# PSUM as eight banks with a fixed plan, and a fixed order of issue, in a sliding-window attention with a gated feed-forward layer

## The chip, the cores and the metric

The kernel runs on one core of a Trainium2 chip. The core has five engines that work side by side, each through its own instructions in order: TensorE (PE in the profile, with its weight loads as PEld), VectorE (DVE), ScalarE (ACT), GpSimd (POOL) and SyncE (SP). POOL and SP also issue the DMA transfers between the memory of the chip (DRAM) and the on-chip buffer (SBUF). Matmuls write to PSUM, a second on-chip buffer of 128 partitions and eight banks; a bank holds 512 fp32 values of each partition. The metric is the device time of one execution in microseconds (us).

## The reference

```python
batch, n_heads, seq, head_dim = (8, 8, 576, 64)          # q, k, v

scores = scale * np.matmul(q, k.transpose(0, 1, 3, 2))    # scale = 1 / sqrt(64)
rel = pos[:, None] - pos[None, :]
slopes = 2.0 ** (-8.0 * (np.arange(H) + 1) / H)
mask = (rel >= 0) & (rel < 128)
scores = np.where(mask, scores - slopes * np.abs(rel), -1e9)
attn = softmax(scores) @ v

x = attn_out.transpose(0, 2, 1, 3).reshape(B * S, H * D)  # 4608 x 512
H = np.maximum(x @ w_h, 0.0)
T = sigmoid(x @ w_t + b_t)
out = T * H + (1.0 - T) * x
```

The inputs and the output are fp32. A query sees itself and the 127 keys before it, with a penalty that grows with the distance.

## The kernel before

**Tiles.** Two batch elements are worked on together (`m` = 0 to 3). The 576 positions of each are four blocks of 128 and a tail of 64. Attention of a pair comes in stages. For m = 1 to 3 they are A (key blocks 0 and 1) and B (2, 3 and the tail); for m = 0 they are the four quarters a, b, c and d. Each stage has eight heads, taken as four pairs `g`. Rows of 128 tokens of a finished stage then go through the feed-forward part, one group at a time: 36 groups in all.

**Pieces.** The work is cut into 763 pieces, called nodes in the code, each of which belongs to one engine:
- On POOL: the loads `qk` (q or k, cast to bf16 while they are moved), `tl` (their tails), `v` (one chunk of 128 keys for both batch elements and all heads, to the tile `VA[m % 2]`), `w` (weights and bias); later `t` (the gate's scaling) and `o` (the output sum).
- On SP: `wf`, the load of w_h in fp32 into a staging area that is the q buffer of m = 1 (`QL[1]`, L215), and the stores `st`.
- On PE: `tr` transposes q (w = 0) or k (w = 1) through PSUM; `s` computes scores of a head (of two heads for m = 0); `pv` multiplies the softmax numerators with V for two heads; `xp` transposes a group of x, `h` and `z` are its two matmuls of 512 columns.
- On ACT: `wc` casts w_h from the staging area to bf16, `te` moves transposes of k from PSUM to SBUF, `exp` is the softmax numerator, `x` moves the transposed x, `th` is the tanh that stands for the sigmoid.
- On DVE: `te` moves transposes of q (and some of k), `msk` multiplies the numerators with the mask, `nrm` divides by the softmax sum, `u` and `g` are parts of the gate, and several memsets and tables of constants run at the start. Among these `ones` (L180) sets the last of the 65 columns that each head has in `VA`, in all five chunks by one memset: the extra column makes `pv` produce the softmax sum. `v` loads fill the other 64 columns of one chunk each.

**Order.** `plan` (L698) is a list scheduler: it holds a cost and a priority for every piece, models buffers, engines and loads, and hands back an order. `SHIFT` and `LOOKS` tune it. The pieces are then issued in that order under `manual_schedule`, so that every engine runs its own pieces in it. A layer below adds the semaphore waits by itself: a piece waits for the earlier pieces that touched the same part of a tile, as far as that layer can tell the parts apart.

**PSUM.** One pool `ps` of four buffers, each of two banks (L78). Every use takes a whole buffer through `ps_tile`: scores of one head, the two transposes of a q and k part (q in the first half, k in the second), and also a group's `xp`, `h` and `z`, which fill one bank of it. A buffer is taken in turn, when the piece that held it four uses earlier is done with it.

**Loads.** The order on POOL's queue before is: q, k, q, k quarters of m = 0; the other halves of q and k of m = 0; q and k of m = 1 whole; w_t, bias; tails of m = 0; V chunks 0 and 1; tails of m = 1; V chunks 2, 3, 4; V of m = 1; q, k and tails of m = 2; V of m = 2; and so on. Eight semaphores serve these transfers in turn, so that a load is issued when the load eight places before it has landed. A load to a buffer that is in use also waits for the last reader.

Of the kernel before, what the change touches and what calls it, by code (L numbers as in the profile page):

```python
# [14 lines left out]
def kernel(  # L15
# [50 lines left out]
        "ps": 4, "pA": 5, "pB": 4, "x": 3, "xt": 5, "uu": 3, "tt": 3, "ot": 3,  # L66
# [11 lines left out]
    psp = ctx.enter_context(tc.tile_pool(name="ps", bufs=BUFS["ps"], space=PSUM))  # L78

    def ps_tile(dt=F32):  # L80
        return psp.tile([P, 2, 512 if dt == F32 else 1024], dt, name="ps")
# [51 lines left out]
    MKA = cp.tile([P, H, 2 * P], BF16, name="mka")  # L133
# [114 lines left out]
    def transposes(m, w, part):  # L248
        i = m % 2
        if w == 0:  # L250
            TR[m, part] = ps_tile(BF16)
        pt = TR[m, part][:, w, :]
# [23 lines left out]
    def evac(m, w, part):  # L276
        i = m % 2
        pt = TR[m, part][:, w, :]
# [24 lines left out]
    def scores(m, kind, h):  # L303
        i, W = m % 2, width(kind)
        if W == 512 or h % 2 == 0:
            SC[m, kind, h] = ps_tile()
        else:
            SC[m, kind, h] = SC[m, kind, h - 1]
# [62 lines left out]

    def pv(m, kind, g):
        va = VA[m % 2]
        av = ps_tile()
# [45 lines left out]
    def f_x(m, kind, gi):  # L420
        bs, n, x = grp(m, kind, gi)
        pt = ps_tile(BF16)
        TR[m, kind, gi] = pt
        for i in range(n):
            for c in range(NCK):
                nc.tensor.transpose(  # L426
                    out=pt[:, i, c * P : (c + 1) * P], in_=x[:, i, c * P : (c + 1) * P],
                    identity=ident[:],
                )

    def f_xe(m, kind, gi):
        n = grp(m, kind, gi)[1]
        xt = fx.tile([P, 2, NCK, P], BF16, name="xt")
        XT[m, kind, gi] = xt
        nc.scalar.copy(  # L435
            out=xt[:, 0:n].rearrange("p i c n -> p i (c n)"), in_=TR[m, kind, gi][:, 0:n, 0:512]
        )

    def f_h(m, kind, gi, i):
        if i == 0:  # L440
            AH[m, kind, gi] = ps_tile()
        for c in range(NCK):
            nc.tensor.matmul(out=AH[m, kind, gi][:, i, :], lhsT=XT[m, kind, gi][:, i, c, :],  # L443
                             rhs=wH[:, c, :], start=c == 0, stop=c == NCK - 1)

    def f_u(m, kind, gi):
# [4 lines left out]
            out=uu[:, 0:n, :], in0=AH[m, kind, gi][:, 0:n, :], scalar=0.0, in1=x,  # L451
# [3 lines left out]
    def f_z(m, kind, gi, i):  # L455
        if i == 0:
            AZ[m, kind, gi] = ps_tile()
        az = AZ[m, kind, gi][:, i, :]
# [5 lines left out]
    def f_th(m, kind, gi):  # L464
# [3 lines left out]
        nc.scalar.activation(out=tt[:, 0:n, :], in_=AZ[m, kind, gi][:, 0:n, :], func=ACTF.Tanh,  # L468
# [34 lines left out]
    nodes = {}  # L503

    def node(key, eng, cost, prio, emit, deps=(), take=None, uses=(), land=0, n=1):


        nodes[key] = (eng, cost, prio, emit, [d for d in deps if d in nodes],
                      take, tuple(uses), land, n)
# [6 lines left out]
    node("ident", "POOL", 500, -120, c_ident)  # L516
    node("trim", "DVE", 300, -110, c_trim)
    node("tri", "POOL", 600, -96.5, lambda: c_tri(0), ["trim"])
    node("tri2", "POOL", 500, -80, lambda: c_tri(1), ["trim"])
    node("cbias", "ACT", 1500, -88, c_bias, ["ident"])  # L520
    node("mka", "DVE", 1300, -95, c_mka, ["tri"])
    node("cvec", "DVE", 1300, -90, c_vec)
    node(("ones", 0), "DVE", 300, -85, lambda: c_ones(0))
    node("mask0", "DVE", 1900, -50, lambda: c_mask(0), ["tri", "cvec"])
    node("mask1", "DVE", 1500, 5 * T, lambda: c_mask(1), ["tri", "tri2", "cvec"])
# [6 lines left out]
    def EV(m, w, part):  # L532
# [4 lines left out]
    HALF = {"A": (330, 1118, 1340, 470, 950), "B": (340, 1118, 1340, 900, 1080),  # L537
            "a": (210, 690, 790, 150, 640), "b": (210, 690, 790, 280, 640),
            "c": (210, 690, 790, 280, 640), "d": (250, 690, 790, 600, 800)}
# [7 lines left out]
    for m in range(ND):  # L547
        p0 = starts[m]
# [11 lines left out]
        def vv(*cs):  # L560
            for c in cs:
                seq.append((("v", m, c), 1150, 2000 if c < 4 else 1000, 1,
# [24 lines left out]
        for n, part in enumerate(parts):  # L587
            for w in (0, 1):
                if part == "tail":
                    src, cost, pr = ("tl", m, w), 450, p0 + (5 if m == 0 else 0 if len(parts) > 5 else -6) * T  # L590
                elif part[0] is None:
                    src, cost, pr = ("qk", m, w, None, None), 580, p0 + (2.4 * n - 12) * T
                else:
                    src, cost = ("qk", m, w, part[0], None if part[0] else part[1]), 1150
# [5 lines left out]
                     [src, "ident"] + [("tr", m, 0, part)] * w, take="ps" if w == 0 else None)  # L600
                node(("te", m, w, part), e, EVC[e][w] if part != "tail" else (420, 590)[e == "ACT"], pr + 1,
                     lambda m=m, w=w, part=part: evac(m, w, part),
                     [("tr", m, w, part)] + last_pv.get(m - 2, []), uses=[("tr", m, 0, part)])
        for kind in ORDER[m]:
            W, U, C = width(kind), UNIT[kind], HALF[kind]
            js = sorted({j for j, _, _ in STAGES[kind]})
            qs = sorted({qb for _, qb, _ in STAGES[kind]})
            for g in range(H // 2):
# [15 lines left out]
                for hl in range(2):  # L624
                    h = 2 * g + hl
                    tk = ("s", m, kind, h if W == 512 else 2 * g)
                    if tk[3] == h:
# [3 lines left out]
                             need + ["mka", "ident"] * add, take="ps")  # L631
                    node(("exp", m, kind, h), "ACT", C[1], tg + (hl - 1.2) * U,
                         lambda m=m, kind=kind, h=h: soft(m, kind, h), [tk, "cbias"] + [("exp", m, kind, 2 * g)] * hl + [owner] * (c0 > 0),
# [3 lines left out]
                if not add:  # L637
                    done = [("msk", key)]
                    node(("msk", key), "DVE", C[2], tg + U, lambda key=key: mask(*key),
                         exps + ["mask0"] + ["mask1"] * (kind in "Bd"), uses=[owner])  # L640
# [5 lines left out]
                     + [("vpad", m % 2)] * (4 in js) + [("v", m, c) for c in vs_], take="ps",  # L646
# [9 lines left out]
            for gi, bs in enumerate(GROUPS[kind]):  # L656
# [4 lines left out]
                if stage_no in DMA_X:  # L661
                    node(("x", kb), "SP", 450 * n, t - 1.3 * dt, lambda kb=kb: f_xd(*kb), alln,
                         take="xt", uses=[xo], land=1000 * n)
                else:
                    node(("xp", kb), "PE", 350 * n, t - 1.0 * dt, lambda kb=kb: f_x(*kb), alln,
                         take="ps", uses=[xo])
                    node(("x", kb), "ACT", (590, 1020)[two], t - 0.9 * dt, lambda kb=kb: f_xe(*kb),
                         [("xp", kb)], take="xt", uses=[("xp", kb)])
                for i in range(n):
                    node(("h", kb, i), "PE", 820, t + 0.4 * i * dt, lambda kb=kb, i=i: f_h(*kb, i),  # L670
                         [("x", kb), ("wc",), ("h", kb, 0)][: 2 + i], take=None if i else "ps",
                         uses=[("x", kb)])
                node(("u", kb), "DVE", (690, 1220)[two], t + 0.2 * dt, lambda kb=kb: f_u(*kb),
                     [("h", kb, n - 1)], take="uu", uses=[("h", kb, 0), xo])
                for i in range(n):
                    node(("z", kb, i), "PE", 1090, t + (0.5 + 0.4 * i) * dt,
                         lambda kb=kb, i=i: f_z(*kb, i),
                         [("x", kb), ("w", 1), ("w", 2)] + [("z", kb, 0)] * i,
                         take=None if i else "ps", uses=[("x", kb)])
# [15 lines left out]
                     lambda kb=kb: f_st(*kb), [("o", kb)], uses=[("o", kb)], land=650 * n)  # L695
            stage_no += 1

    def plan(shift, look):  # L698
        sync, land_ns = 90, 2000
        prio = {key: nd[2] + T * shift.get(key[0] if type(key) is tuple else key, 0.0)  # L700
                for key, nd in nodes.items()}
        when, order = {}, []
        clock = {e: 0.0 for e in ("PE", "ACT", "DVE", "POOL", "SP")}
        held, rings = {}, {r: [] for r in BUFS}
        users, waiting = {}, {}
        for key, nd in nodes.items():
            waiting[key] = len(nd[4])
            for d in nd[4]:
                users.setdefault(d, []).append(key)
            for o in nd[6]:  # L710
                held.setdefault(o, [0, 0.0])[0] += 1

        data = {key: 0.0 for key in nodes}
        ready = {e: [key for key, nd in nodes.items() if nd[0] == e and not nd[4]] for e in clock}
        queue, lanes = 0.0, [0.0] * 8
        while len(order) < len(nodes):
            best = None
            slot = {None: 0.0}
            for r, taken in rings.items():
                slot[r] = 0.0  # L720
                if len(taken) >= BUFS[r]:
                    left, at = held[taken[-BUFS[r]]]
                    slot[r] = None if left else at + sync
            for e in clock:
                cands = []
                for key in ready[e]:
                    nd = nodes[key]
                    s_ = slot[nd[5]]
                    if s_ is None:
                        continue  # L730
                    t = max(clock[e], data[key], s_)
                    if nd[7] and e == "POOL":
                        t = max(t, lanes[nd[8] - 1] + sync)
                    cands.append((t, prio[key], key))
                if cands:
                    t0 = min(c[0] for c in cands) + look[e]
                    c = min((c for c in cands if c[0] <= t0), key=lambda c: c[1])
                    if best is None or c[0] < best[0]:
                        best = c
            assert best, "no piece can start"  # L740
            t, _, key = best
            e, cost, _, _, _, take, uses, land, _ = nodes[key]
            if take:
                rings[take].append(key)
            clock[e] = when[key] = t + cost
            if land:

                shared = 3 * land if queue > t + cost + land else land
                queue = max(queue, t + cost) + land
                when[key] = (queue if e == "POOL" else t + cost + shared) + land_ns  # L750
                if e == "POOL":
# [53 lines left out]
```

The softmax here doesn't subtract the row's maximum and nothing guards it: scores larger than these inputs give would overflow.

## Time and profile before

| | us |
|---|---|
| median of three runs | 185.97 |
| lowest, highest | 184.8, 186.7 |
| the profiled execution | 185.63 |
| its span, first to last instruction | 183.9 |
| ACT exp, 80 instructions (L344) | 73.4 busy |
| PE `h` and `z`, 144 + 144 + 36 matmuls (L443, L460, L462) | 37.2 + 38.0 + 13.9 busy |
| DVE mask, 40 instructions (L363) | 47.8 busy |
| POOL output sum, 35 instructions (L484) | 49.7 busy |

The profile is of one execution; its span is 1.7 us shorter than the time of the same run. A page gives the busy time of each engine, a picture of the span in 40 slices (each digit is a busy share in tenths), the waits by the instruction that waited and the one that released it, the costliest groups of instructions, and the DMA issues with their time to landing. A time line lists instructions with start and duration. Matmul ends are modelled, so the distance of starts in the time line says more of PE's speed than the durations do.

### The profile page before, as it was taken

The page shows a single profiled execution, that of the slowest core. Times are in us where ns is not written, and L with a number is a line of the kernel's source. Part 1 is how long each engine was busy: PE and PEld are TensorE (multiplying, and loading weights), DVE is VectorE, ACT ScalarE, POOL GpSimd, SP SyncE. Part 2 cuts the span into 40 slices and gives each one's busy share as a digit, 9 for nine tenths or more (in the row PEclk, how much of TensorE's full clock was granted, in tenths as well). Part 3 has the DMA queues.
Part 4 walks back from the last instruction along what each step waited for, and adds up shares of the span by engine and source line. Part 5 has one row for each costly group of instructions (what it writes and reads, how often), then busy time and mean ns, then how long its engine had stood idle before and what let it go on. Part 6 is the DMA issues. An engine that isn't in the chain of part 4 may idle for free.

```text
span 183.9 us, 5244 instructions
## 1 busy us (share of the span) xinstructions
PE 155.0 (84%) x2132; PEld 93.9 (51%) x2132; DVE 141.6 (77%) x253; ACT 127.8 (69%) x178; POOL 121.5 (66%) x132
## 2 busy tenths in 40 slices
PE   0286886779999957997999999999998999999950
PEld 0264655655564524675554565665444666555510
DVE  5339885699999893697688999799899788866770
ACT  2558595753889953879779889786998888445510
POOL 7994123979999945984269953544487787667540
PEclk9999999999999996999999999999999999999995
DMA  4999999999999999999997994142212322243543
GB/s 157 225 187 198 200 199 176 138 132 92 127 207 228 210 200 205 135 187 225 208 135 96 178 159 90 45 103 61 57 45 74 93 66 74 74 103 99 137 128 94
DMA packets 70167, 25.50 MB, mean 139 GB/s; under 512 B 48128, under 2 KB 65024, under 8 KB 70144
## 3 DMA queue, kind: packets, MB, share of 16 engines
q0 software_dynamic: 62832, 14.68, 113.6%
q1 hardware_dynamic: 7312, 10.49, 21.3%
q8 instruction: 16, 0.26, 0.6%
q14 instruction: 7, 0.06, 0.1%
HBM read 30.41 MB, written 9.44 MB: 217 GB/s over the span
## 4 chain that ended last, share of the span: by engine, by line
PE 38%; DMA 26%; DVE 16%; POOL 7%; ACT 5%; issue 3%; SPq 1%; POOLq 0%; DVEq 0%; ACTq 0%
DMA kl<-in_k_dram 24%; PE ps L460 10%; PE ps L443 9%; DVE pt L363 6%; PE ps L386 6%; PE ps L270 5%; PE ps L328 5%; DVE x L403 4%; POOL ot L484 3%; DMA out_dram<-ot 3%; ACT pt L344 2%; PE ps L462 2%; DVE uu L450 2%; POOL ql L110 2%; PE ps L426 2%
## 5 line engine op out<-in xcount | busy, mean ns | idle before, releaser
L344 ACT ACTIVATE pt<-ps,bias 128x1024 bf16<-128x1024 f32 (+1 forms) x80 | 73.4, 951 | 9.1 <-PE ps L328 8.4
L484 POOL TENSOR_TENSOR ot<-uu,x 128x512 f32<-128x512 bf16 x35 | 49.7, 1421 | 30.4 <-DVE uu L478 28.9
L363 DVE TENSOR_TENSOR pt<-pt,mk 128x2048 bf16<-128x2048 bf16 (+1 forms) x40 | 47.8, 1210 | 0.7 <-ACT pt L344 0.5
L460 PE MATMUL ps<-wT,xt 128*128 128x512 bf16 x144 | 38.0, 387 | 1.2 <-DVE uu L450 0.7
L443 PE MATMUL ps<-wH,xt 128*128 128x512 bf16 x144 | 37.2, 380 | 0.6 <-DVE uu L450 0.3
L122 POOL DMA_DIRECT2D va<-in_v_dram x20 | 22.2, 1117 | 14.3 <-DMA kl<-in_k_dram 8.2
L450 DVE SCALAR_TENSOR_TENSOR uu<-ps,x 128x512 bf16<-128x512 f32 x36 | 24.8, 688 | 7.7 <-PE ps L443 7.3
L468 ACT ACTIVATE tt<-ps 128x512 f16<-128x512 f32 x36 | 21.5, 598 | 11.6 <-PE ps L462 11.1
L328 PE MATMUL ps<-qt,kt 64*128 64x256 bf16 (+2 forms) x384 | 27.2, 254 | 1.8 <-DVE kt L295 1.4
L473 POOL TENSOR_SCALAR tt<-tt 128x512 f16<-128x512 f16 x32 | 23.1, 722 | 5.6 <-ACT tt L468 5.5
L435 ACT COPY xt<-ps 128x512 bf16<-128x512 bf16 x36 | 21.0, 586 | 8.1 <-PE ps L426 7.2
L403 DVE TENSOR_TENSOR x<-ps,rd 128x256 bf16<-128x256 f32 (+3 forms) x40 | 25.5, 637 | 1.4
L386 PEld LDWEIGHTS <-pt 128*128 128x128 bf16 (+1 forms) x576 | 21.2, 101 | 8.0 <-issue 1.8
L386 PE MATMUL ps<-va,pt 128*128 128x65 bf16 (+1 forms) x576 | 24.1, 196 | 1.3 <-ACT kt L295 0.4
L295 ACT COPY kt<-ps 128x1024 bf16<-128x1024 bf16 x13 | 13.1, 1012 | 14.4 <-PE ps L270 8.4
L289 DVE COPY qt<-ps 128x1024 bf16<-128x1024 bf16 x16 | 10.9, 687 | 14.2 <-PE ps L270 10.9
L478 DVE TENSOR_TENSOR uu<-uu,tt 128x512 bf16<-128x512 bf16 x36 | 16.6, 462 | 4.9 <-POOL tt L473 2.9
L270 PE MATMUL ps<-ident,ql 128*64 128x128 bf16 (+1 forms) x320 | 13.3, 242 | 8.3 <-DMA ql<-in_q_dram 7.5
L443 PEld LDWEIGHTS <-xt 128*128 128x128 bf16 x144 | 12.1, 97 | 14.4 <-issue 2.8
L460 PEld LDWEIGHTS <-xt 128*128 128x128 bf16 x144 | 12.4, 99 | 13.7 <-issue 3.9
L328 PEld LDWEIGHTS <-kt 64*128 64x128 bf16 x384 | 12.8, 97 | 12.6 <-issue 7.0
L270 PE MATMUL ps<-ident,kl 128*64 128x128 bf16 (+1 forms) x320 | 12.8, 242 | 6.6 <-DMA kl<-in_k_dram 5.6
(46 smaller groups left out, 127.9 us busy)
## 6 DMA issues: line engine op xcount, KB each, us to landing
out_dram<-ot SPq DMA_DIRECT2D x128, 64.0 KB, 1.8
va<-in_v_dram POOLq DMA_DIRECT2D x16, 256.0 KB, 10.8
ql<-in_q_dram POOLq DMA_DIRECT2D x3, 1024.0 KB, 14.6
kl<-in_k_dram POOLq DMA_DIRECT2D x3, 1024.0 KB, 18.8
ql<-in_moe_w_h_dram SPq DMA_DIRECT2D x1, 1024.0 KB, 5.8
out_dram<-ot SPq DMA_DIRECT2D x8, 128.0 KB, 2.4
ql<-in_q_dram POOLq DMA_DIRECT2D x4, 128.0 KB, 5.8
kl<-in_k_dram POOLq DMA_DIRECT2D x4, 128.0 KB, 5.9
```

The costliest lines, as they stand in the source:

```text
L122: nc.gpsimd.dma_start(out=VA[m % 2][0:n, c, :, :, 0:D].rearrange("s r h d -> s (r h) d"), in_=v[2 * m : 2 * m + 2, :, c * P : c * P + n, : ...
L270: nc.tensor.transpose(out=pt[r * D : (r + 1) * D, c : c + n], in_=L[ps, r, nh * hs + hl, t * D : (t + 1) * D], identity=ident[ps, ps],)
L328: nc.tensor.matmul(out=sc[:, r, o + off : o + off + w_], lhsT=KT[i][rows, h, j * P : (j + 1) * P], rhs=rhs, start=not add, stop=not add or ...
L344: nc.scalar.activation(out=PT[m, home, h // 2][:, h % 2, :, c0 : c0 + W], in_=SC[m, kind, h][:, :, o : o + W], func=ACTF.Exp, bias=BIAS[:, ...
L363: nc.vector.tensor_tensor(out=o, in0=o, in1=mk.to_broadcast([P, 2, rep, W]), op=ALU.mult,)
L386: nc.tensor.matmul(out=av[rows, hl, n * (D + 1) : (n + 1) * (D + 1)], lhsT=pt[:, hl, r, off : off + (D if narrow else P)], rhs=va[:, j, r, ...
L403: nc.vector.tensor_tensor(out=x.rearrange("p b (h d) -> p h b d", h=2), in0=av[:, :, :, 0:D], in1=rd[:, :, 0:nb].to_broadcast([P, 2, nb, D ...
L443: nc.tensor.matmul(out=AH[m, kind, gi][:, i, :], lhsT=XT[m, kind, gi][:, i, c, :], rhs=wH[:, c, :], start=c == 0, stop=c == NCK - 1)
L450: nc.vector.scalar_tensor_tensor(out=uu[:, 0:n, :], in0=AH[m, kind, gi][:, 0:n, :], scalar=0.0, in1=x, op0=ALU.max, op1=ALU.subtract,)
L460: nc.tensor.matmul(out=az, lhsT=XT[m, kind, gi][:, i, c, :], rhs=wT[:, c, :], start=c == 0, stop=False)
L473: eng.tensor_scalar(out=tt, in0=tt, scalar1=0.5, scalar2=0.5, op0=ALU.mult, op1=ALU.add)
L484: eng.tensor_tensor(out=ot[:, 0:n, :], in0=UU.pop((m, kind, gi))[:, 0:n, :], in1=x, op=ALU.add)
```

## The change

PSUM becomes one tile of eight banks. A piece takes one or two of them, at the place that a list `BANKS` gives for each use in order of issue. Each `tr` piece takes a bank of its own, `xp`, `h` and `z` take one, `pv` takes one for the kinds a to d and two for A and B, scores take two. Scheduler and tuning numbers go; in their place a list `ISSUE` names the pieces in their order. The pieces themselves are the same, but for `mka`, nine DVE instructions that built a table no stage used (`ADD_MASK` is empty), and that is now left out.

```diff
-        "ps": 4, "pA": 5, "pB": 4, "x": 3, "xt": 5, "uu": 3, "tt": 3, "ot": 3,
+        "pA": 5, "pB": 4, "x": 3, "xt": 5, "uu": 3, "tt": 3, "ot": 3,
...
-    psp = ctx.enter_context(tc.tile_pool(name="ps", bufs=BUFS["ps"], space=PSUM))
-
-    def ps_tile(dt=F32):
-        return psp.tile([P, 2, 512 if dt == F32 else 1024], dt, name="ps")
+    psp = ctx.enter_context(tc.tile_pool(name="ps", bufs=1, space=PSUM))
+    PSB = psp.tile([P, 8, 512], F32, name="ps")
+
+    def ps_tile(nb, dt=F32):
+        b = int(next(taken))
+        v = PSB[:, b, :] if nb == 1 else PSB[:, b : b + 2, :]
+        return v if dt == F32 else v.bitcast(BF16)
...
-        if w == 0:
-            TR[m, part] = ps_tile(BF16)
-        pt = TR[m, part][:, w, :]
+        pt = TR[m, w, part] = ps_tile(1, BF16)
...
-            SC[m, kind, h] = ps_tile()
+            SC[m, kind, h] = ps_tile(2)
...
+    def pv_banks(kind):
+        return 1 if len(blocks(kind)) < 4 else 2
...
-        if i == 0:
-            AH[m, kind, gi] = ps_tile()
+        AH[m, kind, gi] = ps_tile(1)
...
-    node("mka", "DVE", 1300, -95, c_mka, ["tri"])
+    if ADD_MASK:
+        node(("mka",), "DVE", 1300, -95, c_mka, [("tri",)])
...
-    order, end = plan(SHIFT, LOOKS)
-
+    names = list(nodes)
+
+    ISSUE = """
+        7 0 16 12 18 3 4 17 9 2 19 6 5 31 24 10 20 35 14 28 32 33 25 34 37 23 51 38 57 52 29 53
...
+    """
+    BANKS = """
+        0 1 2 0 2 4 0 2 6 4 5 2 4 0 1 7 2 4 0 1 7 3 5 7 0 5 2 0 4 7 6 1 3 0 6 3 1 4 2 5 6 0 2 4
...
+    """
+    order = [names[int(n)] for n in ISSUE.split()]
+    taken = iter(BANKS.split())
     with tc.manual_schedule():
-        for t, key in order:
+        for key in order:
             nodes[key][3]()
```

Read as pieces, `ISSUE` gives this beginning on the queues. POOL: q, q, `tri`, k, `ident`, k quarters; q's other half of m = 0; V chunk 0; q's tail; k's other half; bias; k's tail; V chunk 4; w_t; V chunk 1; q and k of m = 1; V chunks 2 and 3; first gates; tails of m = 1; q of m = 2; V chunks 1 and 0 of m = 1 among the first outputs; k and tails of m = 2; V chunks 3, 2 and 4 of m = 1. DVE: tables and masks, three evacuations, mask a of pair 0, `ones` of buffer 0, mask a of pair 1, the next evacuation of q, the first norm. `ones` of buffer 1 comes 59 DVE pieces later, between `u` of group d0 of m = 0 and the mask of pair 1 of stage A of m = 1. ACT: exps of a and the first two of b come ahead of `wc`, which was ACT's first piece. PE: `pv` of a comes ahead of scores b, and so on; pieces of one kind stand together more often, and the groups of a stage no longer go in their order.

## The prediction

> **What bounds the kernel now.** I read first the page's busy shares and its 40 slices of about 4.6 us.
>
> ```profile
> PE 155.0 (84%) x2132; PEld 93.9 (51%) x2132; DVE 141.6 (77%) x253; ACT 127.8 (69%) x178; POOL 121.5 (66%) x132
> ...
> PE   0286886779999957997999999999998999999950
> ...
> DMA  4999999999999999999997994142212322243543
> ```
>
> TensorE (PE) has gaps in the first nine slices and around 65 us, and is full afterwards; DMA is full until slice 22, about 100 us. Then the waits (engine, line, releaser: total us, times, longest) and two windows, cut at 70.6 us, where the second K transposes of batch pair m=2 have run.
>
> ```profile
> PE ps L270 <- DMA ql<-in_q_dram: 7.5, 2, 7.2
> ...
> ACT kt L295 <- DVE qt L289: 6.0, 6, 1.4
> PE ps L270 <- DMA kl<-in_k_dram: 5.6, 3, 3.1
> ...
> PE ps L460 <- DVE uu L450: 0.7, 1, 0.7
> ```
>
> ```profile
> 0.00:70.60 70.60, 51.44 (x843) 33.46 (x845) 53.81 (x115) 46.31 (x72) 49.76 (x64) 1.00 2.18 179
> 70.60:184.00 113.40, 103.61 (x1295) 60.43 (x1289) 87.82 (x138) 81.48 (x106) 71.73 (x68) 0.97 0.84 113
> ```
>
> PE, PEld, DVE, ACT, POOL busy, then clock, DMA share, GB/s. So there are two stages: up to 70.6 us loads decide, PE being busy 51.4 of 70.6 us; from there PE decides, 103.6 of the 106.4 us up to its last end (177.0; 6.9 us of output path follow). PE's waits for PSUM readers are small and scattered: 0.7 us is the longest kind after 39 us except one of 0.8.
>
> PE's own price comes from starts in its timeline:
>
> ```profile
> 57.83 1.04 PE L443 MATMUL ps<-wH,xt 128*128 128x512 bf16 x4
> 58.80 0.39 PE L328 MATMUL ps<-qt,kt 64*128 64x256 bf16 x4
> ...
> 163.24 1.03 PE L443 MATMUL ps<-wH,xt 128*128 128x512 bf16 x4
> 164.10 0.39 PE L426 MATMUL ps<-ident,x 128*128 128x128 bf16 x4
> ```
>
> Four `h` matmuls take 0.86 us to the next start when full-array work follows, 0.97 when scores on half the rows follow: 0.105 us for a change of array shape. The same reading gives `z` 1.08, `xp` 0.22, scores 0.22 a head, `pv` A 0.35 and B 0.74, `tr` of m>0 0.47, tail 0.22.
>
> **What the Trainium skill says.** "Perfetto Trace Analysis", section on the tensor engine instruction, says that "ACT/DVE/GPSIMD are strict FIFO": what stands behind a waiting instruction waits too. The trace agrees: POOL sat 4.3 us before a V load at 70.85 with a gate operation behind it. "DMA: Bandwidth & Descriptors", Specifications, gives 512 B as the least transfer for line rate. V and the tails move 128 B pieces in bf16, q and k 512 B; the windows show 201 GB/s while q and k of m=1 load and 114 GB/s in a stretch of V loads:
>
> ```profile
> 18.60:29.10 10.50, 7.78 (x124) 5.14 (x124) 8.94 (x15) 7.74 (x13) 1.85 (x2) 1.00 1.42 201
> 39.00:50.00 11.00, 10.58 (x137) 6.32 (x134) 10.14 (x26) 6.39 (x12) 10.25 (x10) 1.00 4.59 114
> ```
>
> "TensorE: Matmul & The Clock Gate" (Why this matters for your kernels) warns of PE gaps above about 3 us; after the 3.1 us wait at 66 us the clock line drops to 6 tenths for a slice.
>
> **The change part by part.**
>
> *Banks.* Two halves of a two-bank buffer no longer share a tile: in the program as built, K transposes or evacuations waited for the Q half. That is the 6.0 us of ACT idle above and about 1 us on PE (0.78 at 9.64), all but 0.2 of the latter before 39 us. Buffers for `xp`, `h`, `z` take one bank instead of two. PE's remaining non-DMA excess after 70.6 is 5.6 us (106.4 less 100.8 of priced work, below), so banks can give from 0 to some 4 us; I take 1.
>
> *Array changes.* Counting the pieces in PE's order, 134 changes become 105: 29 x 0.105 = 3.0 us. 24 of them lie after the cut: 2.5 us.
>
> *MKA removed.* Nine DVE instructions, 0.71 + 0.99 us, at 14.6 us. Worth 0: DVE next stands at a wait (below). The extra DVE wait instructions (33 to 69) at the 17 ns that POOL's queue shows for one: 0.6 us on DVE, which has room.
>
> *Loads.* V chunk 0 and tails come ahead of K's second half; q and k of m=1 follow wT; q and k of m=2 come ahead of V of m=1. Landings of before give the prices: quarter q or k 0.65 per issue, half 2.7, whole 5.3 (5.8 to 6.5 beside stores), wT 2.6, a V chunk 2.2, the short one 1.3, a tail pair 1.3; 5 us at least from issue to landing when the queue is empty (5.7 less 0.65).
>
> *Memsets.* Here I put the weight. `ones` (a 0.12 us DVE memset of V's 65th column) ran at 2.3 and 4.2 us, ahead of all V loads:
>
> ```profile
> 2.29 0.12 DVE L180 MEMSET va<- 128x80 bf16 x1 [0.24 <-issue]
> ...
> 4.18 0.12 DVE L180 MEMSET va<- 128x80 bf16 x1 [0.33 <-issue]
> ```
>
> Now `ones/0` follows the issue of V chunks 0 and 4 of m=0, and `ones/1` that of V chunks 3, 2 and 4 of m=1. The column spans all five chunks, and the program as built makes these memsets wait for those transfers to land. Queued behind `ones/0` on DVE: the second mask, the Q evacuation, the first norm; on PE its first `pv` waits for it and all scores behind that; POOL's V chunk 1 too. Behind `ones/1`: the mask of pair 1, the norms and gates of that stage; PE stops at `pv(1,A,0)`; POOL at the next outputs and q of m=3.
>
> First wait: quarters land by 13.3 (k's last issue is 1.5 us later than before), q half 16.0, V0 18.2, tails 19.5, k half 22.3, tails 23.6, V4 24.8. Then `ones` 24.95, mask 0.68, Q evacuation 0.69, scores 0.8, two exps 1.27: 28.4, then the wH cast 1.9. The cast comes behind these exps on ACT now, and q of m=1 lands in wH's staging buffer: it can be issued at 30.3 and lands at 30.3 + 5 + 5.3 = 40.6, against 34.9 if the queue had stayed full.
>
> Second wait: k of m=1 45.9, V2 and V3 50.3, tails 52.9, q of m=2 58.7, V chunks 1 and 0 63.1, k of m=2 69.6, tails 71.6, V3 73.8, V2 76.0, V4 77.3. Cross-check: before, V of m=1 was in by 57.8 with a full queue; q, k and tails of m=2 took from there to 72.2, and the gap of 5.7 makes 77.9. PE reaches `pv(1,A,0)` near 64, DVE `ones/1` near 63, after 16 us of PE pieces behind the k load of 45.9. So PE stands 13 us.
>
> *What is left then.* Before, at 70.6, PE still had 29 `h` 25.1, 29 `z` 31.3, 28 `xp` 6.2, 39 scores 8.6, 14 `tr` 6.6, 4 tails 0.9, 10 `pv` A 3.5, 12 `pv` B 8.9 and 92 changes 9.7: 100.8 us. After, at `pv(1,A,0)`: 25.1, 31.3, 5.9, 43 scores 9.5, 15 `tr` 7.1, 0.9, 12 `pv` A 4.2, 8.9 and 68 changes 7.1: 100.0. The new order brings nearly the same remainder to its release. All early gains sit before that wait and are covered by it; what it is worth is (release - 70.6) - 0.8 + change of PE's idle time.
>
> *Other moves.* SP keeps its 137 issues, wH first; only the stores' order changes with the groups, and POOL waited for a store's landing 1.3 us in all: 0. POOL takes gates and outputs in pairs (t, t, o, o); it is busy 71.7 of 113 us after the cut, so 0. The `tri` pieces (0.61 us on POOL) move ahead of the first k load, which is where k's 1.5 us come from, with trim's later place on DVE; they are in the sum below 13.3 us.
>
> *End.* The last piece is `z` instead of `h`, and tanh 0.60 replaces `u` 0.69 in the final chain: 0.
>
> Sum: 183.9 + (77.5 - 70.6) - 0.8 + 1 = 191.0 us of span. The +1 is the banks' -1 and +2 for a DVE backlog (by its rows about 5 us more is left than before: three masks, two norms, one gate) and a cold restart. What lay around the span was 185.63 - 183.9 = 1.7: 192.7 us. The profiled run is 0.3 below the median 185.97.
>
> **The rivals.**
> *The wait is short, the start pays (faster).* Place: `ones/1` on DVE. If V4 of m=1 lands by 68, only 4 us behind PE's arrival, the span is 183.9 - 2.6 - 0.8 - 1 = 179.5, time 181.2. It decides below a release of 71.4 (at unchanged idle time, the new order is faster below it). For it: V0 lands 18 us earlier, so FFN pieces fill PE's gaps before 39 us; DMA might take mixed small and large packets better than I add them. Against: 114 GB/s in V stretches, and a full queue already gives 72.2. If the queue's gap closes and idle falls by 2, 72.2 gives 182.7, time 184.4: no change.
> *DVE becomes the bound after the release (slower still).* Left on DVE are 87.8 + 5.2 + 0.6 = 93.6 us for about 106 of PE. If masks and evacuations come in bursts, PE's idle time there could double from 5.6 and the release slip to 80: 183.9 + 9.4 - 0.8 + 6 = 198.5, time 200.2.
> *The change doesn't do what it says.* One PSUM tile could be tracked as a whole and everything serialized. The built waits name single banks' users, PE's waits hardly change (DVE 91 to 99, ACT 147 to 136): under 2%.
>
> **How the numbers follow.** Long wait at `ones/1`, PE-bound after: 0.60, 187 to 197. Short wait: 0.17. Near break-even: 0.11. DVE-bound: 0.12. About 1% (184.1 to 187.8) is what can be told from no change. Faster is the short wait's 0.17 less a little, plus some of break-even: 0.17; same 0.11 plus the long wait's low edge: 0.13; slower 0.70. Range 182 to 199: it leaves out half of the short wait and a third of the DVE case. Likeliest: 192.7.
>
> **What would show it.** DVE idle of 5 us or more before the memset of `va` in the first 26 us, and over 8 us before its second one, ending at 74 to 80; PE's largest wait ending with it at L393, about 13 us; PE's own end 105 to 108 us after that. q of m=1 landing near 40. Wrong if the second memset starts before 71, or if PE runs on while it waits.

## The result, and the profile after

| kernel | median, us | to the kernel before | 95% interval |
|---|---|---|---|
| before, beside it | 186.33 | 1 | |
| changed | 194.59 (193.85 to 194.86) | 1.044 | 1.036 to 1.053 |

The change makes the kernel slower by 4.4%. The forecast was 192.7 us, with a range of 182 to 199. The profiled execution of the changed kernel has a span of 193.0 us, against 183.9 before. Of the runs below, the profiled executions of the banks alone, of both controls on the kernel before, and of chunk 4 behind the memset with `ones` of buffer 1 at the start were among the longer ones of their kernels; from these I take waits, order and moments within the execution, while the medians are over all executions of a kernel and the ratios leave the longer ones out.

The page of the changed kernel: busy times, then the slices (4.8 us each now) of PE, of its clock and of DMA.

```profile
PE 150.4 (78%) x2108; PEld 93.0 (48%) x2132; DVE 140.0 (73%) x244; ACT 125.2 (65%) x178; POOL 120.0 (62%) x132
...
PE   0374049999889920699999999999999998999940
...
PEclk9999999999999995599999999999999999999998
...
DMA  5999946999999999979999239799151635244452
```

PE has two holes, in the fourth to sixth slice and in the fifteenth to seventeenth, and is full from there on. Twenty-four of its matmul records are missing, so 150.4 is a little low. In the second hole DMA is at 9: a load is what everything stands for. Two digits of the clock drop to 5 with that hole. (The clock's entries in this trace begin at 37.8 us, so its 9s say nothing of the first hole.) The list of waits gives both holes one name:

```profile
PE ps L393 <- DVE va L183: 18.5, 2, 10.0
...
DVE pt L364 <- DMA va<-in_v_dram: 10.0, 1, 10.0
DVE pt L364 <- DMA wT<-in_moe_w_t_dram: 9.9, 1, 9.9
```

PE waits twice, 18.5 us together, for line 183, the `ones` memset of `VA` (line 180 before). VectorE waits twice, 10 us each, and the profile puts that down to the mask (L364) and to two transfers. The time line shows why the mask is named: the mask is queued behind the memset, but its row starts 0.2 us ahead of the memset's and reaches past it, so the idle time is put down to the mask, first at 25 and then at 78 us.

```profile
25.45 0.87 DVE L364 TENSOR_TENSOR pt<-pt,mk 128x1024 bf16<-128x1024 bf16 x1 [9.91 <-DMA wT<-in_moe_w_t_dram]
25.68 0.12 DVE L183 MEMSET va<- 128x80 bf16 x1
...
78.33 1.41 DVE L364 TENSOR_TENSOR pt<-pt,mk 128x2048 bf16<-128x2048 bf16 x1 [9.99 <-DMA va<-in_v_dram]
78.56 0.12 DVE L183 MEMSET va<- 128x80 bf16 x1
```

On PE, the first `pv` that reads each of the two V tiles starts 0.2 us after its memset:

```profile
25.86 0.40 PE L393 MATMUL ps<-va,pt 128*128 128x65 bf16 x4 [8.45 <-DVE va L183]
...
68.33 0.39 PE L433 MATMUL ps<-ident,x 128*128 128x128 bf16 x4
78.74 0.82 PE L393 MATMUL ps<-va,pt 128*128 128x65 bf16 x12 [10.02 <-DVE va L183]
79.49 0.61 PE L329 MATMUL ps<-qt,kt 64*128 64x256 bf16 x4
80.03 1.89 PE L449 MATMUL ps<-wH,xt 128*128 128x512 bf16 x4
81.85 0.76 PE L329 MATMUL ps<-qt,kt 64*128 64x256 bf16 x8
```

The last row but one shows that PE restarts slowly: four `h` matmuls take 1.82 us to the next start just after the stop, against the 0.86 to 0.97 of the forecast.

### The profile page after: what moved, and what is told of

Same layout as the page of the kernel before. It is cut to its first block, busy times and chain, and to the rows that moved or that the text cites. A ratio compares the mean times of both kernels' runs of the same rounds, so it can differ in the third digit from the quotient of the medians.

```text
span 193.0 us, 5244 instructions
## 1 busy us (share of the span) xinstructions
PE 150.4 (78%) x2108; PEld 93.0 (48%) x2132; DVE 140.0 (73%) x244; ACT 125.2 (65%) x178; POOL 120.0 (62%) x132
## 5 line engine op out<-in xcount | busy, mean ns | idle before, releaser
L345 ACT ACTIVATE pt<-ps,bias 128x1024 bf16<-128x1024 f32 (+1 forms) x80 | 71.6, 948 | 26.5 <-PE ps L329 26.4
L489 POOL TENSOR_TENSOR ot<-uu,x 128x512 f32<-128x512 bf16 x35 | 48.2, 1382 | 28.5 <-DVE uu L483 26.5
L364 DVE TENSOR_TENSOR pt<-pt,mk 128x2048 bf16<-128x2048 bf16 (+1 forms) x40 | 48.2, 1224 | 23.1 <-DMA va<-in_v_dram 10.0
L393 PE MATMUL ps<-va,pt 128*128 128x65 bf16 (+1 forms) x576 | 24.8, 198 | 19.1 <-DVE va L183 18.5
L449 PE MATMUL ps<-wH,xt 128*128 128x512 bf16 x130 | 36.4, 393 | 3.1 <-ACT xt L442 1.8
L465 PE MATMUL ps<-wT,xt 128*128 128x512 bf16 x134 | 36.7, 387 | 2.0 <-DVE x L410 1.2
L410 DVE TENSOR_TENSOR x<-ps,rd 128x256 bf16<-128x256 f32 (+3 forms) x40 | 25.5, 638 | 1.4
L329 PE MATMUL ps<-qt,kt 64*128 64x256 bf16 (+2 forms) x384 | 24.2, 248 | 2.0 <-DVE qt L290 1.7
L465 PEld LDWEIGHTS <-xt 128*128 128x128 bf16 x144 | 13.2, 99 | 16.5 <-issue 4.3
L449 PEld LDWEIGHTS <-xt 128*128 128x128 bf16 x144 | 12.4, 99 | 15.6 <-issue 2.6
L483 DVE TENSOR_TENSOR uu<-uu,tt 128x512 bf16<-128x512 bf16 x36 | 18.2, 520 | 1.8 <-POOL tt L478 1.5
L271 PE MATMUL ps<-ident,ql 128*64 128x128 bf16 (+1 forms) x320 | 11.6, 228 | 8.4 <-DMA ql<-in_q_dram 8.4
L271 PEld LDWEIGHTS <-ql 128*64 128x64 bf16 (+1 forms) x320 | 9.6, 126 | 10.2 <-DMA ql<-in_q_dram 9.2
L467 PE MATMUL ps<-bT,ones 128*128 128x512 bf16 x36 | 13.7, 381 | 0.1
```

Source lines behind the costliest of these rows:

```text
L329: nc.tensor.matmul(out=sc[:, r, o + off : o + off + w_], lhsT=KT[i][rows, h, j * P : (j + 1) * P], rhs=rhs, start=not add, stop=not add or ...
L345: nc.scalar.activation(out=PT[m, home, h // 2][:, h % 2, :, c0 : c0 + W], in_=SC[m, kind, h][:, :, o : o + W], func=ACTF.Exp, bias=BIAS[:, ...
L364: nc.vector.tensor_tensor(out=o, in0=o, in1=mk.to_broadcast([P, 2, rep, W]), op=ALU.mult,)
L393: nc.tensor.matmul(out=av[rows, hl, n * (D + 1) : (n + 1) * (D + 1)], lhsT=pt[:, hl, r, off : off + (D if narrow else P)], rhs=va[:, j, r, ...
L410: nc.vector.tensor_tensor(out=x.rearrange("p b (h d) -> p h b d", h=2), in0=av[:, :, :, 0:D], in1=rd[:, :, 0:nb].to_broadcast([P, 2, nb, D ...
L449: nc.tensor.matmul(out=AH[m, kind, gi], lhsT=XT[m, kind, gi][:, i, c, :], rhs=wH[:, c, :], start=c == 0, stop=c == NCK - 1)
```

## The experiments

Each moves numbers in `ISSUE` or entries of the kernel before's order, and no matmul, transfer or memset is added or left out. In `ISSUE`, 8 and 13 are `ones` of buffer 0 and of buffer 1, and 7 is the first table of VectorE.

### Both memsets, and each alone, at VectorE's start

```diff
-        7 0 16 12 18 3 4 17 9 2 19 6 5 31 24 10 20 35 14 28 32 33 25 34 37 23 51 38 57 52 29 53
-        36 58 54 69 30 63 59 39 8 64 60 55 22 65 40 70 56 21 101 95 71 66 43 96 72 97 67 68 73
...
-        426 281 171 211 210 218 245 172 13 227 277 212 271 179 228 287 219 288 128 272 213 289
+        7 8 13 0 16 12 18 3 4 17 9 2 19 6 5 31 24 10 20 35 14 28 32 33 25 34 37 23 51 38 57 52 29 53
+        36 58 54 69 30 63 59 39 64 60 55 22 65 40 70 56 21 101 95 71 66 43 96 72 97 67 68 73
...
+        426 281 171 211 210 218 245 172 227 277 212 271 179 228 287 219 288 128 272 213 289
```

The second and third kernel move only the 8, and only the 13.

Both:

> The changed kernel with both ones memsets moved back to the start of DVE's queue, everything else as it is. My theory (the memsets' waits for V landings are the loss): the first wait (10.6 us of DVE idle before 25.5 us) goes, q of m=1 lands some 6 us earlier, PE reaches pv(1,A,0) near 62 instead of 68.5 and does not stand there; from there the changed kernel took 193.0 - 78.7 = 114.3 us of span, so a span of 176 to 178 and a time of 175 to 182. Rival A (the order of the loads is at fault, and the memset is only where it shows): PE then stands at the next piece that needs V or q, and the time is 187 to 194. Rival B (banks and a DVE backlog slow the stretch after the release): the stretch after pv(1,A,0) grows by what is saved, 188 or more.

The first alone:

> Only the memset of buffer 0 (m=0) moved back to the start. My theory: the wait before 25.5 us goes and the cast of wH comes earlier, so q of m=1 and all loads behind it land about 6 us earlier, V of m=1 near 72.5; the memset of buffer 1 still holds PE until then. Time 188 to 190, PE's wait at pv(1,A,0) as long as before or longer. Rival A: the release is set by bytes alone and moves by less than 2 us: 192.5 to 194.6.

The second alone:

> Only the memset of buffer 1 (m=1) moved back to the start. My theory: PE does not stop at 68.5 us; V chunks 0 and 1 of m=1 are in by then and chunks 3 and 2 are wanted some 12 us later, when they land. 194.6 less 8 to 10 us: 184.5 to 187. Rival A: PE waits for V at the next pv and no more than 4 us are gained: 190.5 or more.

| moved to the start | median, us | to before | 95% interval | span | start of the first `pv` of m = 1, stage A |
|---|---|---|---|---|---|
| both | 176.89 | 0.961 | 0.949 to 0.972 | 175.8 | 63.3 |
| `ones` of buffer 1 | 183.78 | 0.998 | 0.995 to 1.001 | 182.1 | 69.8 |
| `ones` of buffer 0 | 188.29 | 1.025 | 1.012 to 1.037 | 186.6 | 72.5 |
| none (the changed kernel) | 194.59 | 1.044 | 1.036 to 1.053 | 193.0 | 78.7 |

Two instructions of 0.12 us, moved, turn 4.4% slower into 3.9% faster. Against the kernel with both moved, the first wait alone adds 6.3 us of span (182.1 - 175.8), the second 10.8 (186.6 - 175.8), and both 17.2: they nearly add up. With only the second moved the time came out 0.7 us under the expected range. The page of the kernel with both moved:

```profile
PE 150.6 (86%) x2132; PEld 92.1 (52%) x2132; DVE 141.0 (80%) x244; ACT 124.9 (71%) x178; POOL 120.6 (69%) x132
...
PE   0276489999699999999999999999999999999840
```

PE's second hole is gone. All 2132 matmuls are on record here, as in the kernel before, where they were busy 155.0 us: 4.4 us less for the same matmuls, against 3.0 worked out for the array changes. Why the two waits add up, though the second could have hidden the first, the time of POOL's q load of m = 1 tells, in the changed kernel and with `ones` of buffer 0 moved:

```profile
31.39 1.14 POOL L113 DMA_DIRECT2D ql<-in_q_dram  x1 [4.13 <-ACT wH L228]
```

```profile
24.21 1.14 POOL L113 DMA_DIRECT2D ql<-in_q_dram  x1 [2.66 <-ACT wH L228]
```

It waits for the cast of w_h on ScalarE, and that stands behind exps that stand behind PE's first stop. Every later load follows it on POOL's queue, so the second release came 6.3 us sooner too (72.5 for 78.7). ScalarE in the changed kernel:

```profile
28.05 1.27 ACT L345 ACTIVATE pt<-ps,bias 128x512 bf16<-128x512 f32 x2 [9.68 <-PE ps L329]
29.20 1.90 ACT L228 CAST wH<-ql 128x2048 bf16<-128x2048 f32 x1
```

### The banks alone

The order of the kernel before, with `mka` left out, on the eight banks, each use at the place where the ring of four buffers had it; each transpose piece has its own bank.

```diff
     ISSUE = """
-        7 0 16 12 18 3 4 17 9 2 19 6 5 31 24 10 20 35 14 28 32 33 25 34 37 23 51 38 57 52 29 53
...
+        3 0 16 7 17 8 11 12 18 13 14 19 15 1 2 31 24 6 25 32 33 237 34 35 238 51 36 37
...
     BANKS = """
-        0 1 2 0 2 4 0 2 6 4 5 2 4 0 1 7 2 4 0 1 7 3 5 7 0 5 2 0 4 7 6 1 3 0 6 3 1 4 2 5 6 0 2 4
...
+        0 1 2 4 3 6 0 2 4 6 5 0 7 2 4 6 0 2 4 6 0 3 1 2 4 5 6 0
```

> The order of issue of before (without mka) on the eight banks, each use at the place its ring buffer had, q and k transposes in banks of their own. It shows the banks alone: a gain of 0 to 4 us over before, 182 to 186.5. The waits of ACT's k evacuation for DVE's q evacuation (6.0 us before) should be under 1 us. If the banks bring losses (more waits per instruction), over 187.5.

Measured: 183.82 us, ratio 0.995 (0.992 to 0.999). Its waits of ScalarE at the evacuation of k:

```profile
ACT kt L296 <- PE ps L271: 9.1, 8, 3.5
```

The kernel before had two such rows, one for PE and one of 6.0 us for VectorE's evacuation of q. The second is gone, so the halves no longer wait for each other, and the kernel gains 0.5%, about 0.9 us. The other 3.4 of the 3.9% that the kernel with both memsets at the start gains lie in the new order of issue together with the bank places chosen for it; no run here tells these two apart.

### Controls on the kernel before: a late memset with early V, and with late V

```diff
     order, end = plan(SHIFT, LOOKS)
+    order = [key for _, key in order]
+    order.remove(("ones", 1))
+    order.insert(order.index(("pv", (1, "A", 0))), ("ones", 1))
+    for c in (2, 3, 4):
+        order.remove(("v", 1, c))
+        order.insert(order.index(("qk", 2, 1, None, None)) + c - 1, ("v", 1, c))
...
-        for t, key in order:
+        for key in order:
```

The first control leaves out the three lines of the loop.

> The kernel before, with one instruction moved: the ones memset of m=1 is issued directly ahead of the first pv of m=1, where the changed kernel has it, but behind V loads that in the trace of before landed by about 58 us, some 2 us before VectorE gets there. Theory (what costs is the wait for the V chunks, not the memset): no wait of over 1 us at this memset, ratio .995 to 1.006 to the kernel before. Rival (a late memset is itself dear, or before's order of issue stands so finely that any move costs): over 1.5% slower, with idle time ahead of the first pv of m=1.

> The kernel before, with its ring of banks and its own order of work, in which the ones memset of m=1 is issued directly ahead of the first pv of m=1 and V chunks 2, 3 and 4 of m=1 are issued behind the k load of m=2. Theory (a late memset together with V chunks that land late makes the whole loss, with no need of the new banks or the searched order): VectorE waits at the memset until 68 to 70 us, TensorE stands about 10 us at the first pv of m=1, of which 3.3 us come back because k of m=2 comes sooner; 190 to 193 us. Rival (the loss belongs to the rest of the new order): 184.5 to 187 us.

The late memset alone: 184.88 us, 1.004 (0.999 to 1.008), no change. On VectorE and on PE:

```profile
63.70 0.12 DVE L180 MEMSET va<- 128x80 bf16 x1 [0.24 <-DVE pt L363]
```

```profile
63.89 0.54 PE L386 MATMUL ps<-va,pt 128*128 128x65 bf16 x12 [0.55 <-DVE va L180]
```

With V late as well: 197.33 us, 1.066 (1.056 to 1.075).

```profile
77.57 0.59 DVE L478 TENSOR_TENSOR uu<-uu,tt 128x512 bf16<-128x512 bf16 x1 [14.56 <-DMA va<-in_v_dram]
77.79 0.12 DVE L180 MEMSET va<- 128x80 bf16 x1
```

```profile
77.97 0.84 PE L386 MATMUL ps<-va,pt 128*128 128x65 bf16 x12 [15.08 <-DVE va L180]
```

So the memset's place is harmless in the old order. The late landing by itself is harmless in the new order, as the kernel with both memsets at the start shows; late V alone in the old order was not run. With both, the old order on the old ring loses about 12 us (6.6%), more than the expected 190 to 193 us. My size for it was wrong: I had the release at 68 to 70 us, when k of m = 2 lands, but the three V loads stand behind that load, and at 2.2 us each (1.3 for the short one) they end at 74 to 76. It came at 77.6, as the first row shows.

### The loads that the second memset waits for, moved

V chunks 3, 2 and 4 of m = 1 (244, 243, 245) go ahead of k of m = 2 (413):

```diff
-        197 260 248 253 192 241 143 186 161 261 121 83 144 149 249 155 162 123 413 84 150 134
+        197 260 248 253 192 241 143 186 161 261 121 83 144 149 249 155 162 123 244 243 245 413 84 150 134
...
-        206 193 254 269 194 244 138 425 176 275 207 243 276 255 177 270 127 208 280 178 217 209
-        426 281 171 211 210 218 245 172 13 227 277 212 271 179 228 287 219 288 128 272 213 289
+        206 193 254 269 194 138 425 176 275 207 276 255 177 270 127 208 280 178 217 209
+        426 281 171 211 210 218 172 13 227 277 212 271 179 228 287 219 288 128 272 213 289
```

> The changed kernel with both late memsets, but V chunks 3, 2 and 4 of m=1 issued ahead of the k load of m=2. Theory: the last V chunk lands some 6.5 us of load plus 2 us of tails earlier, the second memset is released near 70 us in place of 78.5, TensorE stands 2 to 4 us there in place of 10.0, and 186 to 189 us come out. If it turns out that TensorE then waits for the k transposes of m=2 instead, up to 191. Rival (the wait at the second memset hangs on something other than when V lands): 193 to 195 us and a release at 78 us again.

Measured: 190.24 us, 1.029 (1.022 to 1.036), with a span of 188.1 us for the changed kernel's 193.0: better, but not the 186 to 189 us. The memset no longer waits for a transfer: the trace counts the last V chunk as landed (all updates of its semaphore in) at 71.3 us, and the memset runs at 75.6 only because VectorE gets to it then. PE and VectorE stand a little earlier, for something else. PE, VectorE and POOL between 59 and 69 us:

```profile
68.58 1.07 PE L271 MATMUL ps<-ident,ql 128*64 128x128 bf16 x16 [6.05 <-DVE x L410]
```

```profile
65.36 2.47 DVE L483 TENSOR_TENSOR uu<-uu,tt 128x512 bf16<-128x512 bf16 x1 [3.29 <-POOL tt L478]
```

```profile
59.95 0.69 POOL L118 DMA_DIRECT2D ktl<-in_k_dram  x1 [1.79 <-DMA ql<-in_q_dram]
60.64 0.64 POOL L478 TENSOR_SCALAR tt<-tt 128x512 f16<-128x512 f16 x1
61.97 0.71 POOL L118 DMA_DIRECT2D qtl<-in_q_dram  x1 [0.69 <-DMA va<-in_v_dram]
64.00 0.68 POOL L118 DMA_DIRECT2D qtl<-in_q_dram  x1 [1.32 <-DMA va<-in_v_dram]
64.69 0.63 POOL L478 TENSOR_SCALAR tt<-tt 128x512 f16<-128x512 f16 x1
```

Read from the bottom: POOL can't issue the tails before earlier loads have landed, since eight semaphores serve all of them; the gate operation at 64.69 stands behind; VectorE's gate waits for it; the norm (L410) stands behind that one, and PE's transposes wait for the norm. "Perfetto Trace Analysis" of the Trainium skill, section on the tensor engine instruction, calls the queues of these two engines strictly first in, first out; the trace agrees, POOL and VectorE each passing on a wait that was not theirs, until it is 6.05 us on PE. To see whether that is the whole cause, the four tail loads go behind the gate operations on the same queue (414 and 415 behind 169):

```diff
-        156 187 124 135 264 259 94 163 415 173 122 164 201 265 188 266 262 125 202 165 198 414
-        203 263 167 174 166 267 204 199 256 200 168 205 257 126 169 273 268 136 175 274 170 137
+        156 187 124 135 264 259 94 163 173 122 164 201 265 188 266 262 125 202 165 198
+        203 263 167 174 166 267 204 199 256 200 168 205 257 126 169 415 414 273 268 136 175 274 170 137
```

> The changed kernel with V chunks 3, 2 and 4 of m=1 ahead of k of m=2, as in the run with that edit alone (190.2 us), and with the four tail loads of m=2 moved on POOL's queue behind the three gate operations (line 478) that stood between them there. Theory (what was left of the second stall there was POOL waiting to issue tail loads, with gate operations behind it that VectorE and then TensorE waited for): TensorE's wait of 6.1 us at the q transposes near 62 to 68 us falls under 3 us, the gate operation that ended POOL's stretch at 65.3 us ends before 61.5 us, and 186 to 188.5 us come out. Rival (what is left is the late memset itself, or TensorE waits for k of m=2 anyway): 189.5 to 191.5 us.

Measured: 187.66 us, 1.020 (1.009 to 1.030), span 186.3, inside the theory's range. PE's longest stop there and the gate operation, which ended at 62.2 rather than under 61.5:

```profile
67.61 1.02 PE L465 MATMUL ps<-wT,xt 128*128 128x512 bf16 x4 [1.99 <-DVE uu L456]
```

```profile
61.54 0.62 POOL L478 TENSOR_SCALAR tt<-tt 128x512 f16<-128x512 f16 x1 [1.94 <-ACT tt L473]
```

The gate operation now waits for ScalarE and not for loads. So the second wait could be removed by the order of the loads alone, at the price of five pieces moved, where moving the one memset does more (183.78 us).

### What the first memset waits for

The profile names the w_t transfer as what released the first memset. By the program's order w_t (22) is issued behind the memset (8), ahead of it only V chunks 0 and 4 of m = 0. In the first kernel chunk 4 (30) goes behind the memset; in the second also the 13 goes to VectorE's start; in the third everything stays, but w_t goes behind V chunk 1 (21), whose issue waits for the memset.

```diff
-        36 58 54 69 30 63 59 39 8 64 60 55 22 65 40 70 56 21 101 95 71 66 43 96 72 97 67 68 73
+        36 58 54 69 63 59 39 8 30 64 60 55 22 65 40 70 56 21 101 95 71 66 43 96 72 97 67 68 73
```

```diff
-        36 58 54 69 30 63 59 39 8 64 60 55 22 65 40 70 56 21 101 95 71 66 43 96 72 97 67 68 73
+        36 58 54 69 30 63 59 39 8 64 60 55 65 40 70 56 21 22 101 95 71 66 43 96 72 97 67 68 73
```

> The changed kernel, with V chunk 4 of m=0 issued behind the ones memset of m=0, so that this memset waits for V chunk 0 alone; the memset of m=1 stays late. Theory (V chunk 4 is what held the first memset until 25.5 us): released near 20 us, first pv by 21 us, q of m=1 issued near 25 us; the second wait stays, about 10 us long, ending near 72 us as in the run with the first memset early; 187.5 to 190 us. Rival (the weight transfer that the profile names as the releaser is what held it): still released at 25 us, 193 to 195 us.

> The changed kernel with both waits taken away by different means: V chunk 4 of m=0 issued behind the memset of m=0, which itself stays late, and the memset of m=1 at VectorE's start. Theory (only what the memsets wait for costs, so that this is nearly the kernel with both memsets at the start, 176.9 us, less 1 us since q of m=1 was issued at 26.4 here against 25.3 us there): 176.5 to 180 us, no wait over 3 us at either memset. Rival (a late memset of m=0 costs by where it stands, as in the run with the memset of m=1 alone at the start, 183.8 us): 181.5 to 184.5 us.

> The changed kernel with one load moved: w_t is issued behind V chunk 1 of m=0, which itself waits for the first memset, so that w_t cannot be on its way before the memset runs. Both late memsets and all V loads stay where they are. Theory (V chunk 4 of m=0 holds the first memset; the profile's label, the w_t transfer, names the wrong transfer): memset again between 24 and 26.5 us, TensorE's stop there 7 to 9.5 us, 192.5 to 196 us. Rival (w_t is what held it): memset before 22 us, and a time as with V chunk 4 behind the memset, 188 to 191.5 us.

| kernel | median, us | to before | 95% interval | first memset at |
|---|---|---|---|---|
| V chunk 4 behind the memset | 190.65 | 1.032 | 1.022 to 1.041 | 20.7 |
| the same, and `ones` of buffer 1 at the start | 178.20 | 0.968 | 0.958 to 0.977 | 20.5 |
| w_t behind V chunk 1 | 193.83 | 1.050 | 1.039 to 1.061 | 23.6 |

With chunk 4 behind it the memset is released 5 us sooner. The time is 0.65 us above the expected 187.5 to 190: q of m = 1 was issued at 26.4 rather than near 25, and the second release came at 75.5, not near 72. POOL issues w_t after chunk 4, so that move made w_t late too, and only the third kernel tells the two apart:

```profile
23.82 0.40 PE L393 MATMUL ps<-va,pt 128*128 128x65 bf16 x4 [6.58 <-DVE va L183]
```

```profile
15.48 0.82 POOL L125 DMA_DIRECT2D va<-in_v_dram  x1 [1.15 <-DMA ql<-in_q_dram]
24.05 1.17 POOL L125 DMA_DIRECT2D va<-in_v_dram  x1 [7.75 <-DVE va L183]
25.21 0.76 POOL L234 DMA_DIRECT2D wT<-in_moe_w_t_dram  x1
```

w_t is issued at 25.2, and PE had still stopped for 6.6 us (7 to 9.5 expected), until 23.8, before it could be on its way. Chunk 4, issued at 15.48 here and at 16.59 in the changed kernel, is what the memset waited for, and the label was wrong. The changed kernel's own trace agrees: it counts chunk 4 as landed at 25.3 us, just ahead of the memset, and w_t only at 27.2, behind it. The release came 0.4 us before the expected stretch and 2.0 us before the changed kernel's. Chunk 4 was issued 1.1 us earlier, and chunk 0 too landed 2.0 us earlier here (17.3 for 19.3), before w_t was issued in either kernel, so the rest need not be w_t's doing. The time of the second kernel shows that most of the first wait can be removed without touching the memset: PE still stops 3.4 us at its first `pv` (over 3 was not expected), and 2.5 us with both memsets at the start, for V chunk 0.

## Why the prediction was right

**The two waits: right in place, and within about 1 us in time.** The first memset started at 25.68 (24.95 forecast), the second at 78.56 (77.5 to release). On the way to the first, two errors partly cancel: the quarters were in at 11.8, 1.5 us sooner than forecast, but V chunk 4 landed at 25.3 (24.8). The trace counts most of the later loads as landed close to their forecast: q of m = 1 at 40.7 (40.6), k of m = 1 at 46.2 (45.9), q of m = 2 at 58.9 (58.7), k of m = 2 at 68.9 (69.6), V chunk 3 at 73.4 (73.8). The late microsecond comes at the end: chunk 2 landed 3.7 us behind chunk 3, where 2.2 were reckoned, at 77.1, and chunk 4 at 78.1 (77.3).

**PE's stop: 10.0 us, not 13.** The mis-sized term is PE's arrival. I had it at 64 us, 16 us of pieces behind a k load of m = 1 at 45.9; PE began the transposes of that k at 49.1 and ended the last piece ahead of `pv` at 68.7. It changed nothing, since the release sets the end. That can be read off the runs: span less the start of that `pv` is 114.3 us in the changed kernel, 114.1 with `ones` of buffer 0 moved, 114.4 with chunk 4 behind the memset and 113.9 with w_t moved. These four have a stop of 7.5 us or more there. Where PE came without one it is 112.5 (both moved), 112.3 (`ones` of buffer 1 moved, with or without chunk 4 behind the first memset) and 112.3 (V ahead of k, where PE had stopped and restarted before it). With the tails moved as well it is 114.1 without such a stop, but there PE stands 1.7 us for k of m = 2 a little later, at 76.5 to 78.2.

**The remainder and the restart.** PE's own end was at 186.5, 107.8 us after its release; 105 to 108 was forecast, and 106.6 in the sum. The difference between 114.2 and 112.4 is what the stop costs beyond its own length, 1.8 us. The granted clock (third number from the end) accounts for it: it is halved from 72.0 us, 3.2 us into the stop, to 82.2 us.

```profile
71.90:78.70 6.80, 0.00 (x0) 0.00 (x0) 0.37 (x2) 0.00 (x0) 0.00 (x0) 0.50 1.91 180
78.70:82.20 3.50, 3.46 (x24) 1.50 (x25) 2.17 (x4) 1.11 (x1) 1.20 (x2) 0.50 1.05 144
```

About 3.5 us of work at half clock lose some 1.7 us. "TensorE: Matmul & The Clock Gate" of the Trainium skill (Why this matters for your kernels) puts the drop at idle gaps above about 3 us; this stop agrees, but it is no sharp limit here: with w_t moved, the clock was also halved from 52.7 to 56.1 us, right behind a stop of only 2.2 us.

I had put the restart together with a backlog of VectorE at 2 us, and there the forecast was lucky. The restart was no new cost: the kernel before ran at half clock from 70.4 to 73.8 us, after its 3.1 us wait. The window after the release shows no backlog on top:

```profile
78.70:187.00 108.30, 103.17 (x1323) 61.75 (x1340) 92.36 (x142) 83.11 (x109) 73.76 (x70) 0.98 0.82 111
```

VectorE is busy 92.4 of 108.3 us, PE 103.2 (its missing matmul records not counted), and behind the first `pv` PE waits for VectorE for only 1.0 us in all, so the rival in which VectorE becomes the bound falls. But the remainder itself was mis-sized. Before, it was 106.4 us, or about 104.8 without the time lost at half clock; less the forecast's 0.8 and 1 that makes 103.0. With both memsets at the start, at full clock throughout, PE needs 106.1 us from that `pv` to its end. The 2 us happened to cover most of these 3 us; where they come from, no run here shows.

**The sum.** Forecast span 191.0, measured 193.0: +1.2 from the release (`pv` at 78.7 for 77.5), +1.2 from PE's remainder, and the path from PE's end to the last store 6.5 instead of 6.9, -0.4. In the profiled execution 1.9 us lay around the span instead of 1.7 (194.82 - 192.96), and it took 0.2 more than the median.

**Banks, array changes, the rest.** Banks were taken at 1 us and measured at 0.9, at the old ring's places. For the array changes 3.0 us were worked out; 4.4 fewer busy microseconds were measured, in a kernel that also has no restart. At some 1.7 us for the restart before, 2.7 are left, near 3.0, but the split is argued. The rival that one PSUM tile is tracked as a whole falls with the vanished row of 6.0 us. What the rival of a short wait said, that the order pays once the release is early enough, holds: its break-even at 71.4 agrees with 183.9 - 112.4 = 71.5 for an arrival without a stop; after a stop, it is 183.9 - 114.2 = 69.7. PE could have been there at 63.3.

**What the forecast missed** is how much lay covered. It said that the early gains sit before the second wait; it did not say that with both memsets at the start the same order would be 7 to 8 us faster than the kernel before.

## What to carry to other kernels

When an order of issue is rearranged, list first the instructions whose waits change in kind: a cheap write that shares a tile with transfers is free ahead of them and waits for all of them behind them. A wait at one place is worth its whole chain: here the first one delayed a cast, the cast a load, and that load the second wait, so that both came to be paid in full. Order two things on a queue of transfers by who stands behind them on the issuing engine too, since an engine that cannot issue a load holds up its arithmetic.

## What the runs showed beyond that

- The releaser that a profile names for a wait on several transfers can be a transfer that was no part of it: in the changed kernel w_t was named, and with w_t moved out of the way the wait stayed (6.6 us of PE).
- A stop of TensorE of 7.5 to 10.6 us cost about 1.8 us more than its length in four kernels: the granted clock stayed at half for 3.3 to 4.8 us after PE had started again.
- POOL, with loads in flight on all eight semaphores, stood 1.8, 0.7 and 1.3 us at three tail loads of 64 KB; three V loads moved ahead of them were enough for that.
